# Row sums for the token groups by wide matmuls and 32 by 32 transposes, with the output groups taken in token order

## The chip, the cores and the metric

One core of one Trainium2 chip. The metric is the device time of one execution in microseconds (us); lower is better. The kernel before takes 180.8 us. Its executions agree within 0.3%, so a change of 0.5 us can be seen.

## The reference, cut to what matters

The program is a windowed attention followed by a "soft mixture of experts". Attention gives a matrix `x` of 4608 tokens (8 batches of 576) by 512. Then:

```python
logits = x @ phi                                  # 4608 x 32 slots
d = softmax of logits over the tokens             # axis 0
slot_out = for each expert e: relu((d.T @ x)[e] @ w1[e]) @ w2[e]     # 32 x 512
c = np.exp(logits - logits.max(1, keepdims=True))
c /= c.sum(1, keepdims=True) + 1e-09              # row sums: one per token
return (c @ slot_out).astype(np.float32)          # 4608 x 512
```

The change touches the last two lines: how the row sums of `c` are formed, and in which groups of 512 tokens the result is computed and stored.

## The kernel before

`o_et` holds `exp(logits)` transposed, 32 slots over the partitions and tokens along the free dimension. A small list scheduler in the kernel orders all operations; each gets a priority (`prio`, from the table `OFFS` and from `PERIOD`), and it keeps track of which operation reads or writes which buffer (`reads=`, `writes=`). The program gives each engine its instructions in the order that it finds.

The output is made in nine groups of 512 tokens. 576 is not a multiple of 512, so groups 0 to 7 are the first 512 tokens of each batch, and group 8 collects the last 64 tokens of all eight batches ("tail"). Its result goes back to eight places in the output:

```python
    op(POOL, lambda: pool.tensor_copy(                       # gather of the tail tokens
        a(o_tail, [[4, 8], [32, 16], [1, 4]]), a(o_et + 512, [[576, 8], [4, 16], [1, 4]])), ...)
    # row sums: a 33rd column in the matmul ET of each batch, and a matmul RS for the tail
    ...
    def tok(G, j):
        return (a(o_et + 576 * G + j, [[4, 128]]) if G < 8 else a(o_tail + j, [[4, 128]]))
    ...
    def store(G, c0, cw, prio, j0=0, n=4):
        ...
        if G < 8:
            dst = out[576 * G:576 * G + 512, c0:c0 + cw].rearrange("(p j) f -> p j f", j=4)[:, j0:j0 + n, :]
            src = af(ostg(G) + 2 * (512 * j0 + c0), [[512, n], [1, cw]])
        else:
            dst = out.rearrange("(b r) f -> b r f", b=8)[:, 512:576, :].rearrange("b (i j) f -> i b (j f)", j=4)
            src = af(ostg(G), [[1, 2048]])
        store_ops.append(op(SP, lambda: spq.dma_start(dst, src), ...))
    ...
    NA = 2.5         # the first 2.5 groups are stored by column halves, while the last weights land
    for G, x in [(2, 2)] + [(G, x) for G in (8, 3, 4, 5, 6, 7) for x in (0, 2)]:
        ...          # the other groups, 1 MB a store; group 8 goes first of the six
```

In every full store a partition holds four tokens, 8 KB that lie together in the output. For groups 0 to 7 the output side of the transfer is 128 pieces with one step. For group 8 it is 16 times 8 pieces: partition 8i+b goes to piece i of batch b.

The softmax here doesn't subtract the row's maximum and nothing guards it: scores larger than these inputs give would overflow.

## Time and profile before

| | before |
|---|---|
| time, median | 180.82 us |
| span of the profiled execution | 179.0 us |
| last weight packet ends | 152.3 us |
| loop over the attention ends, first L1 matmul | 129.2 us |
| 8 KB store packets: first start, last end | 160.45 us, 178.22 us |
| first 128 of them: mean duration | 518 ns |
| the others: median duration | 309 ns |

L1 and L2 are the first and the second matmul layer of the experts (`w1`, `w2`). The packet figures are read from the DMA records of the trace (start, size and duration of each packet of the queue that stores use), not from a printed view; the records do not say which of the 16 DMA engines moved a packet. The span of the profiled execution is 1.8 us shorter than its time.

The page shows the span in 40 slices. The DMA row is the busy share of the 16 DMA engines in tenths, the other what they moved in GB/s:

```profile
DMA  6999999999999999999999999999999999899996
GB/s 185 234 213 210 217 207 215 211 211 210 218 207 213 215 209 210 215 210 210 215 208 212 213 211 217 211 215 210 219 209 217 196 195 230 304 356 264 421 419 260
```

The DMA engines are busy from the first slice to the last (6 tenths in these two, 8 or 9 in all the others). While loading they write some 212 GB/s into the core; inputs are read as float32 and written as bfloat16, so an estimated 424 GB/s are read. The page's totals bear out the factor of about two: 61.93 MB read from HBM, 31.8 MB written into the core (41.26 MB moved less 9.44 MB of stores). In the stores at the end the rate reaches 421 GB/s, but one slice (161 to 165.6 us) has only 264.

The end of the chain of waits (start, duration, what):

```profile
120.53 32.06 DMA ar<-in_moe_w_dram
152.59 0.04 issue
152.63 0.30 PE ps L857
152.95 0.44 DVE ar L881
153.89 8.63 DVE ar L913 x15
```

The last load is waited for until 152.6 us; compute adds little after it, and then results are evicted and stored. The timeline of PE shows how much room the second layer (line 857) has:

```profile
136.14 4.28 PE L857 MATMUL ps<-ar 128*32 128x512 bf16 x44 [0.45 <-DVE ar L842]
141.93 1.04 PE L857 MATMUL ps<-ar 128*32 128x512 bf16 x4 [1.51 <-DMA ar<-in_moe_w_dram]
144.50 1.05 PE L857 MATMUL ps<-ar 128*32 128x256 bf16 x8 [1.53 <-DMA ar<-in_moe_w_dram]
```

In brackets is the idle time before each and what ended it: PE waits for weights, 1.51 and 1.53 us, so a microsecond more or less of compute before this costs nothing. Last, the windows view in the store phase; after the window and its length come the busy times of PE (the matmul engine), PEld (its weight loads), DVE (vector engine), ACT (scalar engine) and POOL (GpSimd), then the PE clock, the DMA share, and GB/s:

```profile
160.00:161.00 1.00, 0.96 (x4) 0.24 (x4) 1.00 (x2) 1.00 (x3) 0.00 (x0) 1.00 1.13 328
161.00:162.00 1.00, 0.93 (x5) 0.23 (x3) 1.00 (x3) 1.00 (x3) 0.00 (x0) 1.00 1.08 238
162.00:163.00 1.00, 0.33 (x1) 0.03 (x1) 1.00 (x2) 1.00 (x3) 0.00 (x0) 1.00 0.84 172
163.00:164.00 1.00, 0.00 (x0) 0.00 (x0) 1.00 (x3) 0.22 (x1) 0.00 (x0) 1.00 1.10 336
177.00:178.00 1.00, 0.00 (x0) 0.00 (x0) 0.00 (x0) 0.00 (x0) 0.00 (x0) 0.50 0.35 147
```

From 160 to 163 us the DMA engines are busy (a packet counts where it starts, so a share can pass 1: 1.13, 1.08, 0.84) but slow. That is when the first 1 MB store, group 8, runs.

### The profile page before, as it was taken

Reading aid. Unit: us, or ns where it says so; the run is one execution under the profiler, and the core shown is the slowest. Engines: PE = TensorE matmul, PEld = TensorE weight load, DVE = VectorE, ACT = ScalarE, POOL = GpSimd, SP = SyncE. Lnnn points to the kernel's source line nnn. Section 1 sums busy time; section 2 is a strip of 40 time slices with the busy share of each in tenths; the row PEclk is TensorE's granted clock in tenths of the full one; section 3 lists DMA queues with packets and bytes.
Section 4 is the critical chain, followed back from the end, with each engine's and each line's share of the span. In section 5 each row is a group of like instructions: output and inputs, shape, how many; then the busy total and the mean of one; then the engine's idle time right before and its main releaser. Section 6 shows DMA issues by size and latency. Waiting matters only on the chain.

```text
span 179.0 us, 4780 instructions
## 1 busy us (share of the span) xinstructions
PE 127.9 (71%) x2093; PEld 87.5 (49%) x2094; DVE 118.0 (66%) x220; ACT 104.7 (58%) x165; POOL 51.7 (29%) x103
## 2 busy tenths in 40 slices
PE   0009778989789989989699989976697657892000
PEld 0006556666567767767477767664444224420000
DVE  6898579788899899899589699383300015797000
ACT  2405299797789799798666889875111004694000
POOL 7559741332423432333930000790100000000000
PEclk9999999999999999999965999999879999999555
DMA  6999999999999999999999999999999999899996
GB/s 185 234 213 210 217 207 215 211 211 210 218 207 213 215 209 210 215 210 210 215 208 212 213 211 217 211 215 210 219 209 217 196 195 230 304 356 264 421 419 260
DMA packets 19220, 41.26 MB, mean 230 GB/s; under 512 B 1920, under 2 KB 8576, under 8 KB 18304
## 3 DMA queue, kind: packets, MB, share of 16 engines
q0 software_dynamic: 15056, 30.41, 90.0%
q1 hardware_dynamic: 4144, 10.55, 16.6%
q8 instruction: 16, 0.26, 0.5%
q14 instruction: 4, 0.03, 0.0%
HBM read 61.93 MB, written 9.44 MB: 399 GB/s over the span
## 4 chain that ended last, share of the span: by engine, by line
DMA 32%; PE 23%; DVE 23%; ACT 6%; POOL 4%; issue 2%; DVEq 0%
DMA ar<-in_moe_w_dram 18%; DMA ar<-in_k_dram 15%; PE ps L509 7%; DVE ar L488 6%; DVE ar L913 6%; ACT ar L548 4%; POOL ar L371 4%; PE ps L603 3%; DVE ar L614 3%; PE ps L570 3%; PE ps L516 2%; PE ps L526 2%; PE ps L693 2%; DVE ar L494 2%; DVE ar L445 2%
## 5 line engine op out<-in xcount | busy, mean ns | idle before, releaser
L548 ACT ACTIVATE ar<-ps 128x1152 bf16<-128x1152 f32 (+1 forms) x32 | 38.0, 1186 | 22.8 <-PE ps L533 12.5
L488 DVE STREAM_TRANSPOSE ar<-ar 128x576 uint32<-128x576 uint32 x40 | 48.4, 1240 | 3.1 <-DMA ar<-in_k_dram 2.9
L509 PE MATMUL ps<-ar 128*128 128x320 bf16 (+1 forms) x128 | 23.9, 313 | 15.4 <-DVE ar L488 13.1
L614 DVE TENSOR_TENSOR ar<-ps,fs 96x768 bf16<-96x768 f32 (+1 forms) x32 | 26.3, 823 | 1.2
L576 ACT ACTIVATE ar<-ps 128x768 bf16<-128x768 bf16 x32 | 24.8, 811 | 2.2 <-PE ps L570 2.2
L509 PEld LDWEIGHTS ps<-ar 128*128 128x128 bf16 x128 | 10.9, 102 | 20.1 <-POOL ar L418 13.1
L603 PE MATMUL ps<-ar 128*128 128x65 bf16 x320 | 15.7, 200 | 3.4 <-ACT ar L548 3.1
L570 PE MATMUL ps<-ar 128*128 128x128 bf16 x192 | 16.3, 232 | 2.2 <-DVE ar L614 1.9
L910 ACT ACTIVATE ar<-ps,fs 128x512 f32<-128x512 f32 (+1 forms) x23 | 11.4, 641 | 8.3 <-PE ps L901 8.3
L603 PEld LDWEIGHTS ps<-ar 128*128 128x128 bf16 x320 | 12.9, 101 | 6.3 <-ACT ar L548 3.8
L335 POOL DMA_DIRECT2D ar<-in_k_dram x16 | 8.9, 553 | 23.1 <-DVE ar L488 18.2
L610 DVE RECIPROCAL fs<-ps 96x12 f32<-96x12 f32 (+1 forms) x32 | 6.4, 200 | 12.6 <-PE ps L603 12.4
L570 PEld LDWEIGHTS ps<-ar 128*128 128x128 bf16 x192 | 12.8, 120 | 3.6 <-DVE ar L614 2.4
L857 PE MATMUL ps<-ar 128*32 128x512 bf16 (+1 forms) x80 | 10.5, 338 | 5.0 <-DMA ar<-in_moe_w_dram 3.5
L913 DVE TENSOR_SCALAR ar<-ps,fs 128x512 f32<-128x512 f32 (+1 forms) x23 | 12.7, 628 | 1.0 <-PE ps L901 1.0
L364 POOL DMA_DIRECT2D ar<-in_moe_w_dram x12 | 6.4, 580 | 22.2 <-DVE ar L488 22.2
L335 POOL DMA_DIRECT2D ar<-in_q_dram x16 | 8.7, 546 | 11.5 <-DVE fs L610 6.6
L335 POOL DMA_DIRECT2D ar<-in_v_dram x16 | 8.8, 549 | 9.2 <-DVE fs L610 5.5
L670 ACT ACTIVATE ar<-ps 128x576 bf16<-128x576 bf16 x16 | 9.6, 652 | 2.3 <-PE ps L654 2.3
L901 PE MATMUL ps<-ar 128*128 128x512 bf16 (+1 forms) x45 | 9.8, 339 | 1.5 <-DVE ar L881 1.0
L693 PE MATMUL ps<-ar 128*128 128x288 bf16 x64 | 9.2, 287 | 1.2 <-ACT ar L677 1.2
L857 PEld LDWEIGHTS ps<-ar 128*32 128x32 bf16 x80 | 4.7, 96 | 10.6 <-DMA ar<-in_moe_w_dram 6.8
(75 smaller groups left out, 192.6 us busy)
## 6 DMA issues: line engine op xcount, KB each, us to landing
ar<-in_moe_w_dram POOLq DMA_DIRECT2D x29, 512.0 KB, 27.2
out_dram<-ar SPq DMA_DIRECT2D x6, 1024.0 KB, 11.0
ar<-in_k_dram POOLq DMA_DIRECT2D x16, 288.0 KB, 21.8
ar<-in_q_dram POOLq DMA_DIRECT2D x16, 288.0 KB, 22.3
ar<-in_v_dram POOLq DMA_DIRECT2D x16, 288.0 KB, 22.3
out_dram<-ar SPq DMA_DIRECT2D x10, 256.0 KB, 3.8
ar<-in_moe_w_dram SPq DMA_DIRECT2D x1, 1024.0 KB, 4.9
ar<-in_moe_w_dram POOLq DMA_DIRECT2D x2, 256.0 KB, 31.7
```

The costliest lines, as they stand in the source:

```text
L335: return pool.dma_start(a(o_stg + (s * 3 + j) * 1152, [[1, 1152]]), src[b, 4 * dl:4 * dl + 4].rearrange("h (p t) d -> (h p) (t d)", p=32))
L488: return dve.transpose(au(o_dst, [[1, 18], [18, 32]]), au(src, [[32, 18], [1, 32]]))
L509: pe.matmul(pf(h, 0, [[1, W]]), a(o_id, [[1, 128]]), a(msk, [[1, W]]), start=True, stop=False)
L548: eo = op(ACT, lambda P=P, W=W: act.activation(a(P, [[W, 4], [1, W]]), AP(ps, 0, [[4096, 128], [512, 4], [1, W]]), ACTF.Exp, scale=SCALE), ...
L570: last = pe.transpose(pb(bank.idx, bb * 256 + par * 32, [[64, 4], [1, 32]]), src, a(o_id, [[1, 128]]))
L576: op(ACT, lambda t=t, bank=bank: act.activation(a(o_vb[vs] + 3 * t * VBK, [[66, 12], [2, 32], [1, 2]]), pb(bank.idx, 0, [[64, 12], [1, 32] ...
L603: last = pe.matmul(pf(bank.idx + x, 65 * t, [[1, 65]]), w, a(VB + t * VBK + 66 * h, [[1, 65]]), start=True, stop=True)
L614: op(DVE, lambda hp=hp, bank=bank: dve.tensor_tensor(a(ox + 128 * hp, [[64, 2], [256, NT], [1, 64]], 0, rows), pf(bank.idx, 0, [[512, 2], ...
L693: last = pe.matmul(pf(bank.idx, 0, [[1, 288]]), a(o_phis + 128 * c, [[1, 128]]), a(o_xt[xt] + 576 * c + 288 * g, [[1, 288]]), start=(c == ...
L857: last = pe.matmul(pf(sobank[x].idx, 0, [[1, n]], 32 * j, 32), a(o_htz + 1024 * g + 128 * c + 32 * j, [[1, 32]]), a(w2off(e) + DM * c + co ...
L910: op(ACT, lambda: act.activation(dst, src(), ACTF.Copy, scale=sca), actt(cw, .1), prio + .1, reads=[bank, b_rinv], writes=wr, name=f"OE{G} ...
L913: op(DVE, lambda: dve.tensor_scalar(dst, src(), sca, None, op0=AluOp.mult), dvet(cw, True) + .08, prio + .1, reads=[bank, b_rinv], writes= ...
```

## The change

The intent: take groups of 512 consecutive tokens over the borders of the batches, so that the gather, the tail buffer and the scattered store go. The row sums then no longer fit the batches. They are made three groups at a time: four matmuls of 384 columns, each to its own 32 partitions, with weights of 32 equal columns, so that every output row is the row sum; a 32 by 32 transpose on DVE is to bring the tokens into the partitions. `OFFS` and `PERIOD`, the priorities of the scheduler, were retuned.

```diff
-PERIOD = 20.3
+PERIOD = 21.8
-OFFS = dict(T=54.1, SC=81.0, EX=-15.2, MK=68.9, ...)
+OFFS = dict(T=92.2, SC=104.1, EX=-30.5, MK=78.7, ...)
 ...
-                last = pe.matmul(pf(bank.idx, 33 * t, [[1, 33]]), w, a(o_sel, [[1, 33]]),
+                last = pe.matmul(pf(bank.idx, 32 * t, [[1, 32]]), w, a(o_sel, [[1, 32]]),
 ...
-        op(DVE, lambda bank=bank: dve.reciprocal(
-            f(o_rinv + 4 * b, [[1, 4]]), pf(bank.idx, 33 * 6 + 32, [[33, 4]])), ...)
 ...
+    def row_sums(g0, g1, prio):
+        ...
+                for qd in range(4):
+                    last = pe.matmul(pf(bank.idx + m, 0, [[1, 384]], 32 * qd, 32), a(o_rm, [[1, 32]]),
+                                     a(o_et + 512 * (g0 + 3 * m) + 128 * qd, [[512, 3], [1, 4], [4, 32]]),
+                                     start=True, stop=True)
+        op(PE, fn, pet(4 * n, 384), prio, reads=[b_et, b_rm], writes=[bank], name=f"RS{g0}")
+        op(DVE, lambda: dve.transpose(af(o_rt, [[384, n], [1, 384]]), pf(bank.idx, 0, [[512, n], [1, 384]])), ...)
+        op(DVE, lambda: dve.reciprocal(f(o_rinv + 4 * g0, [[1, 12 * n]]), af(o_rt, [[32, 12 * n]])), ...)
 ...
+        if i in (9, 13):
+            row_sums(0 if i == 9 else 3, 3 if i == 9 else 6, 15 * PERIOD)
 ...  (tail gather, RS and RR8 removed)
+    row_sums(6, 9, T1 + 4)
 ...
-        if G < 8:
-            dst = out[576 * G:576 * G + 512, c0:c0 + cw].rearrange(...)
-        else:
-            dst = out.rearrange("(b r) f -> b r f", b=8)[:, 512:576, :].rearrange("b (i j) f -> i b (j f)", j=4)
+        dst = out[512 * G:512 * G + 512, c0:c0 + cw].rearrange("(p j) f -> p j f", j=4)[:, j0:j0 + n, :]
 ...
-    for G, x in [(2, 2)] + [(G, x) for G in (8, 3, 4, 5, 6, 7) for x in (0, 2)]:
+    for G, x in [(2, 2)] + [(G, x) for G in range(3, 9) for x in (0, 2)]:
```

More of the change, by code (lines that the diff above doesn't have):

```diff
@@ L26 @@
 LRU = 130.0
-OFFS = dict(T=54.1, SC=81.0, EX=-15.2, MK=68.9, TB=-27.8, VE=-19.3, PV=-25.0, RC=-26.6,
-            NM=-144.9, XT=-17.3, XE=7.3, LG=-85.5, EXL=22.3, ET=33.1, EE=23.9, SI=46.0, SA=37.9)
+OFFS = dict(T=92.2, SC=104.1, EX=-30.5, MK=78.7, TB=-29.0, VE=-46.3, PV=-36.7, RC=-26.4,
+            NM=-241.3, XT=-17.7, XE=8.2, LG=-77.2, EXL=95.9, ET=37.3, EE=30.2, SI=61.8, SA=58.7)
 class Buf:
@@ L240, in bass_dilated_sliding_attn__then__soft_moe_slots_kernel @@
     o_id = take(128)
-    o_sel = take(34)
-    o_rm = o_sel + 32
+    o_sel = take(32)
+    o_rm = take(32)
+    o_rt = take(768)
     o_so = take(512)
-    o_tail = take(512)
     o_htz = take(2 * 8 * 4 * 32)
@@ L310, in bass_dilated_sliding_attn__then__soft_moe_slots_kernel @@
     b_w2h = [[Buf(f"w2h{x}{s}") for s in range(2)] for x in range(4)]
-    b_htz, b_tail, b_so = Buf("htz"), Buf("tail"), [Buf("soA"), Buf("soB")]
+    b_htz, b_rt, b_so = Buf("htz"), Buf("rt"), [Buf("soA"), Buf("soB")]
     b_hsb = [Buf(f"hsb{x}") for x in range(2)]
@@ L457, in const_ops @@
            reads=[b_sel], writes=[b_rm])
+        op(DVE, lambda: dve.tensor_copy(a(o_rm + 1, [[1, 31]]), a(o_rm, [[0, 31]])), .1, D0 + 1, rmw=[b_rm])
     const_ops()
@@ L720, in half @@
         ek = b % 2
-        op(PE, et_fn, pet(11, 33), pr("ET"), reads=[b_et, b_sel, b_rm], writes=[bank], name=f"ET{b}")
-        ee = op(ACT, lambda bank=bank: act.activation(
-            a(o_ek[ek], [[32, 11], [1, 32]]), pf(bank.idx, 0, [[33, 11], [1, 32]]), ACTF.Copy), actt(352),
-           pr("EE"), reads=[bank], writes=[b_ek[ek]], name=f"EE{b}")
-        op(DVE, lambda bank=bank: dve.reciprocal(
-            f(o_rinv + 4 * b, [[1, 4]]), pf(bank.idx, 33 * 6 + 32, [[33, 4]])), .2, pr("EE") + .1,
-           reads=[bank], writes=[b_rinv], after=[ee], name=f"RR{b}")
+        op(PE, et_fn, pet(11, 32), pr("ET"), reads=[b_et, b_sel], writes=[bank], name=f"ET{b}")
+        op(ACT, lambda bank=bank: act.activation(
+            a(o_ek[ek], [[1, 352]]), pf(bank.idx, 0, [[1, 352]]), ACTF.Copy), actt(352), pr("EE"),
+           reads=[bank], writes=[b_ek[ek]], name=f"EE{b}")
         bank = Bank(f"si{b}")
@@ L750, in half, with fn @@
            rmw=[b_sid] if b < 7 else [], writes=[b_sdb] if b == 7 else [], name=f"SD{b}")
-    def tok(G, j):
-        return (a(o_et + 576 * G + j, [[4, 128]]) if G < 8 else
-                a(o_tail + j, [[4, 128]]))
+    def row_sums(g0, g1, prio):
+        n = (g1 - g0) // 3
+        bank = Bank(f"rs{g0}", n)
+        def fn():
+            last = None
+            for m in range(n):
+                for qd in range(4):
+                    last = pe.matmul(pf(bank.idx + m, 0, [[1, 384]], 32 * qd, 32), a(o_rm, [[1, 32]]),
+                                     a(o_et + 512 * (g0 + 3 * m) + 128 * qd, [[512, 3], [1, 4], [4, 32]]),
+                                     start=True, stop=True)
+            return last
+        op(PE, fn, pet(4 * n, 384), prio, reads=[b_et, b_rm], writes=[bank], name=f"RS{g0}")
+        op(DVE, lambda: dve.transpose(af(o_rt, [[384, n], [1, 384]]), pf(bank.idx, 0, [[512, n], [1, 384]])),
+           .1 + .4 * n, prio + .1, reads=[bank], writes=[b_rt], name=f"RT{g0}")
+        op(DVE, lambda: dve.reciprocal(f(o_rinv + 4 * g0, [[1, 12 * n]]), af(o_rt, [[32, 12 * n]])),
+           .2, prio + .2, reads=[b_rt], writes=[b_rinv], name=f"RR{g0}")
     last_ex = [None]
@@ L794, in bass_dilated_sliding_attn__then__soft_moe_slots_kernel @@
        reads=[bank], writes=[b_sit], name="sid")
-    op(POOL, lambda: pool.tensor_copy(
-        a(o_tail, [[4, 8], [32, 16], [1, 4]]), a(o_et + 512, [[576, 8], [4, 16], [1, 4]])), .8, T1 + 4, reads=[b_et],
-       writes=[b_tail], name="tail")
-    bank = Bank("rs")
-    def rs_fn(bank=bank):
-        last = None
-        for j in range(4):
-            last = pe.matmul(pf(bank.idx, j, [[1, 1]]), tok(8, j), a(o_rm, [[1, 1]]),
-                             start=True, stop=True)
-        return last
-    op(PE, rs_fn, pet(4, 72), T1 + 4, reads=[b_tail, b_rm], writes=[bank], name="RS")
-    op(DVE, lambda bank=bank: dve.reciprocal(f(o_rinv + 32, [[1, 4]]), pf(bank.idx, 0, [[1, 4]])),
-       .2, T1 + 4.2, reads=[bank], writes=[b_rinv], name="RR8")
+    row_sums(6, 9, T1 + 4)
     for x in range(2):
@@ L900, in out_tile @@
         rd = [b_so[s] for s in range(2) if c0 < 256 * (s + 1) and c0 + cw > 256 * s]
-        op(PE, lambda: pe.matmul(pf(bank.idx, 0, [[1, cw]]), tok(G, j),
+        op(PE, lambda: pe.matmul(pf(bank.idx, 0, [[1, cw]]), a(o_et + 512 * G + j, [[4, 128]]),
                                  a(o_so + c0, [[1, cw]]), start=True, stop=True),
-           pet(1, cw), prio, reads=[b_et if G < 8 else b_tail] + rd, writes=[bank], name=f"O{G}{j}{c0}")
+           pet(1, cw), prio, reads=[b_et] + rd, writes=[bank], name=f"O{G}{j}{c0}")
         dst = af(ostg(G) + 2 * (512 * j + c0), [[1, cw]])
@@ L919, in store @@
               if c0 < 256 * (s + 1) and c0 + cw > 256 * s]
-        if G < 8:
-            dst = out[576 * G:576 * G + 512, c0:c0 + cw].rearrange("(p j) f -> p j f", j=4)[:, j0:j0 + n, :]
-            src = af(ostg(G) + 2 * (512 * j0 + c0), [[512, n], [1, cw]])
-        else:
-            dst = out.rearrange("(b r) f -> b r f", b=8)[:, 512:576, :].rearrange("b (i j) f -> i b (j f)", j=4)
-            src = af(ostg(G), [[1, 2048]])
+        dst = out[512 * G:512 * G + 512, c0:c0 + cw].rearrange("(p j) f -> p j f", j=4)[:, j0:j0 + n, :]
+        src = af(ostg(G) + 2 * (512 * j0 + c0), [[512, n], [1, cw]])
         store_ops.append(op(SP, lambda: spq.dma_start(dst, src), .1, prio, kind="dma",
@@ L939, in bass_dilated_sliding_attn__then__soft_moe_slots_kernel @@
         store(G, 256, 256, T2 + 10 + G + .25 * x + .2, x, 2)
-    for G, x in [(2, 2)] + [(G, x) for G in (8, 3, 4, 5, 6, 7) for x in (0, 2)]:
-        at = G if G < 8 else 2.6
+    for G, x in [(2, 2)] + [(G, x) for G in range(3, 9) for x in (0, 2)]:
         for j in (x, x + 1):
-            out_tile(G, j, 0, 512, T2 + 10 + at + .1 * x)
+            out_tile(G, j, 0, 512, T2 + 10 + G + .1 * x)
         if G < NA:
-            store(G, 0, 512, T2 + 10 + at + .1 * x + .1, x, 2)
+            store(G, 0, 512, T2 + 10 + G + .1 * x + .1, x, 2)
         elif x:
-            store(G, 0, 512, T2 + 10 + at + .3)
+            store(G, 0, 512, T2 + 10 + G + .3)
     order = sc.run([4, 5, 6, 7], [0, 1, 2, 3], last_ex[0])
```

## The prediction

> **What bounds the kernel now.** The DMA queues, nearly from first to last. In the page's 40 slices the DMA row is at 9 between the first slice and the last, except one 8. The windows view gives 212 GB/s into the core from 10 to 140 us (written as bf16, so about 424 GB/s read as float32), 191 to 196 GB/s in the column slabs of the last two experts, then 410 to 440 GB/s of stores. [...] The chain of waits says the same: its last loading step is a weight DMA, 120.5 to 152.6 us, then L2, eviction, stores. The timeline ends the compute loop about 128 us; L2 of the first experts is done at 140.4, then waits 1.5 us for weights at 141.9 and again at 144.5. So compute has slack: over 1 us in the tail, far more in the loop, where a load takes 22 us from issue to landing.
>
> **What the change does.**
> - PE: ET gets 32 instead of 33 columns (nothing). Twelve matmuls of 384 columns with 32 output rows come, four at a time over the array's columns. L1, the same form, does 64 of 512 columns in 4.97 us, so my estimate is 0.7 us in all[...]. The old RS (0.30 us) goes.
> - DVE: eight reciprocals of 0.16 to 0.18 us go; three transposes of 128x384 come, 0.8 us each by an estimate from 1.16 us for 128x576, and three small reciprocals. Net about +1.5 us, 0.9 us of it after the loop, where DVE waits anyway.
> - POOL: the 0.63 us gather of the tail tokens goes. It was off the chain.
> - The loop's order is retuned. I expect its end to move by up to 2 us, the load end not at all.
> - Stores: still six of 1 MB and eleven smaller, but the ninth group is no longer 128 pieces of 8 KB scattered over eight batches. This is on the critical path. In the trace's DMA records the 8 KB store packets take 309 ns in the median; the first 64, from 160.45 us, about 600 to 640 ns, and 32 of the next 64 about 530. By issue order these 128 are the scattered group. Their excess, over 16 engines, is 1.7 us; throughput at 162 to 163 us falls to 172 GB/s. [...]
>
> **Sum.** Load end unchanged, 152.6 us. Stores from 160.4 us: six times 2.46 us plus what is left of contention, ending about 176.5 instead of 178.2. Everything else is hidden. Predicted 179.2 us, range 178.2 to 180.9. Faster by over 2%: 0.03; within 2%: 0.94; slower by over 2%: 0.03.
>
> **What would show it.** 8 KB store packets at 309 ns from the first on; no slice under 300 GB/s between 160 and 164 us; last weight landing within 0.5 us of 152.6; L2 still waiting for weight DMA; RS under 1.5 us of PE; three transposes about 0.8 us each.
>
> **What would make it wrong.** (1) The slow packets come from the evictions beside them until 164.5 us, not from the scattered rows: then the next group is slow and nothing is gained (about 180.8). (2) The last row sums land before the last slot sums and push L1 and L2 past the weights: over 1.5 us shows as later first stores. (3) The row sums read the buffer that the next batch's exponentials write, so they stall the loop; over several us this starves the load queue.

Stores from 160.4 us, six times 2.46 us (128 packets of 309 ns over 16 engines are 2.47), and by difference 1.3 us for what is left of contention, end at 176.5 us. In the kernel before, the last store packet ends at 178.22 us in the trace and the time is 180.82; with these 2.6 us the sum comes to 179.1.

## The result, and the profile after

The kernel after takes 178.31 us (median of 4 runs, 178.13 to 178.71) against 180.85 us. The ratio is 0.986, 95% interval 0.984 to 0.988. Ratios here are the mean time of one kernel's fast runs over that of the other's fast runs of the same rounds, so not quite the ratio of the medians quoted. All these runs are fast (an execution over 1.5% above the fastest of its kernel is called slow and left out).

| | before | after |
|---|---|---|
| span | 179.0 us | 176.3 us |
| first L1 matmul | 129.2 us | 128.1 us |
| last weight packet ends | 152.3 us | 152.2 us |
| 8 KB store packets: first start, last end | 160.45, 178.22 us | 160.32, 175.54 us |
| first 128 of them: mean duration | 518 ns | 318 ns |
| sum of all their durations, over 16 engines | 16.83 us | 15.13 us |

The same lines after. First the slices:

```profile
DMA  5999999999999999999999999999999999999997
GB/s 182 237 211 213 216 207 213 214 209 213 215 208 214 214 208 214 214 207 215 210 209 213 211 211 216 213 216 210 217 213 211 210 192 194 298 319 415 416 427 316
```

The slice of 264 GB/s is gone; from 158.7 us on all but the last are at 415 or more. The chain of waits has the same end, at the same times, within 0.1 us:

```profile
119.16 33.35 DMA ar<-in_moe_w_dram
152.51 0.04 issue
152.56 0.30 PE ps L858
152.88 0.44 DVE ar L882
153.81 8.63 DVE ar L914 x15
```

So at most 0.13 us was gained before the stores: the first 8 KB packet starts at 160.32 instead of 160.45 us. The windows of the store phase:

```profile
154.00:155.00 1.00, 1.00 (x8) 0.66 (x7) 1.00 (x4) 1.00 (x4) 0.00 (x0) 1.00 0.59 206
160.00:161.00 1.00, 0.96 (x4) 0.16 (x3) 1.00 (x2) 1.00 (x3) 0.00 (x0) 1.00 1.11 455
161.00:162.00 1.00, 0.93 (x4) 0.26 (x3) 1.00 (x3) 1.00 (x3) 0.00 (x0) 1.00 0.99 401
162.00:163.00 1.00, 0.25 (x1) 0.00 (x0) 1.00 (x2) 1.00 (x3) 0.00 (x0) 1.00 1.05 434
163.00:164.00 1.00, 0.00 (x0) 0.00 (x0) 1.00 (x3) 0.16 (x1) 0.00 (x0) 1.00 0.99 410
```

DVE still evicts at full load until 164 us and ACT until 163 us, and still the stores run at over 400 GB/s. The added work, from the groups by shape (busy time and mean of one in ns, then idle time before it):

```profile
L760 PE MATMUL ps<-ar 128*32 128x384 bf16 x12 | 1.7, 501 | 0.0
L766 DVE STREAM_TRANSPOSE ar<-ps 128x384 f32<-128x384 f32 x3 | 1.7, 571 | 1.9 <-PE ps L760 1.9
L768 DVE RECIPROCAL fs<-ar 128x12 f32<-128x12 f32 x3 | 0.7, 222 | 0.1
```

The four matmuls of a set overlap; a set takes 0.51 us, three sets 1.5 us. Other forecasts held too: the last weight lands at 152.2 us, and L2 still waits for weight DMA (1.23 us before 141.77 us, by the timeline).

Two things call for an explanation. The sum of the packets' durations fell by 1.70 us (16.83 - 15.13), as predicted, but the stretch from the first to the last of them fell by 2.55 us (17.77 - 15.22). And nothing so far says why the scattered store was slow.

### The profile page after: what moved, and what is told of

Same layout as the page of the kernel before. It is cut to its first block, busy times and chain, and to the rows that moved or that the text cites. A ratio compares the mean times of both kernels' runs of the same rounds, so it can differ in the third digit from the quotient of the medians.

```text
span 176.3 us, 4802 instructions
## 1 busy us (share of the span) xinstructions
PE 126.7 (72%) x2102; PEld 85.4 (48%) x2102; DVE 119.6 (68%) x218; ACT 104.3 (59%) x165; POOL 51.1 (29%) x102
## 4 chain that ended last, share of the span: by engine, by line
DMA 47%; DVE 21%; PE 13%; POOL 4%; ACT 4%; issue 2%; POOLq 0%; DVEq 0%
DMA ar<-in_k_dram 28%; DMA ar<-in_moe_w_dram 19%; DVE ar L489 6%; DVE ar L914 6%; PE ps L510 4%; POOL ar L371 3%; ACT ar L549 3%; PE ps L604 2%; DVE ar L615 2%; PE ps L571 2%; DVE ar L445 2%; PE ps L517 2%; DVE ar L450 1%; PE ps L527 1%; DVE ar L495 1%
## 5 line engine op out<-in xcount | busy, mean ns | idle before, releaser
L510 PE MATMUL ps<-ar 128*128 128x320 bf16 (+1 forms) x128 | 23.4, 308 | 15.7 <-DVE ar L489 13.8
L510 PEld LDWEIGHTS ps<-ar 128*128 128x128 bf16 x128 | 10.4, 100 | 20.8 <-POOL ar L418 13.7
L571 PE MATMUL ps<-ar 128*128 128x128 bf16 x192 | 15.8, 228 | 2.8 <-DVE ar L615 1.9
L604 PEld LDWEIGHTS ps<-ar 128*128 128x128 bf16 x320 | 12.8, 100 | 6.5 <-ACT ar L549 3.8
L858 PE MATMUL ps<-ar 128*32 128x512 bf16 (+1 forms) x80 | 11.4, 352 | 5.9 <-DMA ar<-in_moe_w_dram 5.2
L571 PEld LDWEIGHTS ps<-ar 128*128 128x128 bf16 x192 | 12.4, 118 | 4.3 <-DVE ar L615 2.5
L902 PE MATMUL ps<-ar 128*128 128x512 bf16 (+1 forms) x46 | 10.4, 356 | 1.3 <-DVE ar L882 1.0
```

The lines of the kernel that those rows point to most:

```text
L510: pe.matmul(pf(h, 0, [[1, W]]), a(o_id, [[1, 128]]), a(msk, [[1, W]]), start=True, stop=False)
L571: last = pe.transpose(pb(bank.idx, bb * 256 + par * 32, [[64, 4], [1, 32]]), src, a(o_id, [[1, 128]]))
L604: last = pe.matmul(pf(bank.idx + x, 65 * t, [[1, 65]]), w, a(VB + t * VBK + 66 * h, [[1, 65]]), start=True, stop=True)
L858: last = pe.matmul(pf(sobank[x].idx, 0, [[1, n]], 32 * j, 32), a(o_htz + 1024 * g + 128 * c + 32 * j, [[1, 32]]), a(w2off(e) + DM * c + co ...
L902: op(PE, lambda: pe.matmul(pf(bank.idx, 0, [[1, cw]]), a(o_et + 512 * G + j, [[4, 128]]), a(o_so + c0, [[1, cw]]), start=True, stop=True), ...
```

## The experiments

Theory S: the whole gain comes from the store of the ninth group; the rest of the change is neutral. Rivals: E, the evictions beside the first 1 MB store made it slow; R, the new row sums and order have a part. On why the store is slow: A, its addresses are far apart; P, its form, that is, which partition goes to which piece (16 times 8 instead of one step of 128), wherever the pieces lie.

Five of the kernels below (`b_contig`, `a_scatter`, `b_perm`, `b_pitch`, `b_pitchperm`) put rows in the wrong order. The comparison with the reference passed them all the same: the rows of this result differ little (any entry is within 3.1e-5 of its column's mean, where the largest entry is 4.4e-4), so it cannot see the order of rows. For the kernels that are called correct here, the kernel after among them, the order rests on reading the code.

### 1. Before, with contiguous stores

```diff
-        if G < 8:
-            dst = out[576 * G:576 * G + 512, ...]
-        else:
-            dst = out.rearrange(...)           # the eight places
+        dst = out[512 * G:512 * G + 512, c0:c0 + cw].rearrange("(p j) f -> p j f", j=4)[:, j0:j0 + n, :]
```

> The kernel before, with every group's store at a contiguous 1 MB of the output (rows 512G to 512G+511), all else as before; the result is wrong on purpose. Theory S (the scattered rows of the ninth group's store are the whole gain): 178.1 to 178.6 us, 8 KB store packets at 309 ns from the first on, and the last ones end within 0.5 us of one another. Rival E (the evictions that run beside the first 1 MB store slow it, wherever it goes): 180.8 us, first 128 packets still slow. Rival R (part of the gain comes from the rest of the change): about 179.2 us, the gain from the packets' mean excess alone (1.7 us).

Measured: 178.37 us, ratio to before 0.9859 (0.9842 to 0.9875), the same as the kernel after. One of its four executions took 369.8 us and counts as slow; the profile fell on it, so of this kernel only the three fast times (178.14 to 178.49) are used. What the forecast says of single packets could therefore not be checked in it. With nothing but the stores changed, the whole gain is there. For the ninth group that is two things at once, its addresses and the form of the transfer (one step of 128 instead of 16 times 8); experiments 4 to 6 take them apart.

### 2. After, with the stores addressed as before

```diff
+        if G != 3:
+            at = 576 * (G if G < 3 else G - 1)
+            dst = out[at:at + 512, ...]
+        else:
+            dst = out.rearrange(...)           # the eight places
```

> The kernel after, with its stores addressed as before: the first 1 MB group goes to the eight 64-row holes, the others to rows 576k; the result is wrong on purpose. Theory S: 180.6 to 181.0 us, the first 128 packets of 8 KB at about 600 ns. Rival E: unchanged, 178.3 us. Rival R: about 180.0 us, since the new row sums and the new order keep their part.

Measured: 180.74 us against 180.77, ratio 0.9996 (0.9981 to 1.0011). The first 64 packets of 8 KB have a median of 624 ns, and the windows view shows the slow stretch again:

```profile
162.00:163.00 1.00, 0.25 (x1) 0.00 (x0) 1.00 (x2) 1.00 (x3) 0.00 (x0) 1.00 0.99 229
```

The new row sums, the new order and the missing gather together are worth nothing that these runs can tell; S stands, R and E fall.

### 3. Before, with the scattered group last

```diff
-    for G, x in [(2, 2)] + [(G, x) for G in (8, 3, 4, 5, 6, 7) for x in (0, 2)]:
-        at = G if G < 8 else 2.6
+    for G, x in [(2, 2)] + [(G, x) for G in (3, 4, 5, 6, 7, 8) for x in (0, 2)]:
+        at = G
```

> The kernel before, the scattered group stored last of the six instead of first; correct result. Theory S: the slow packets move to the end of the stores (after 175 us), the first 1 MB store is at 309 ns; the time stays at 180.8 or grows by up to 1 us[...]. Rival E: the first 1 MB store (now a contiguous one) stays slow, the scattered one is at 309 ns, time 180.8 us.

Measured: 180.09 us, ratio 0.9958 (0.9943 to 0.9973), result correct. The slow packets went with the group: the first 128 take 318 ns in the mean, the last 128 take 487. The windows view, beside the evictions and long after them:

```profile
162.00:163.00 1.00, 0.23 (x1) 0.00 (x0) 1.00 (x2) 1.00 (x2) 0.00 (x0) 1.00 1.03 426
174.00:175.00 1.00, 0.00 (x0) 0.00 (x0) 0.00 (x0) 0.00 (x0) 0.00 (x0) 0.50 1.03 188
```

E is refuted a second time: the first store is fast beside the evictions, and the last is slow where none runs. It got 0.7 us faster, not slower as I had thought possible: the packets add up to less (16.61 us over 16 engines instead of 16.83), and an engine is idle for less of the last 2.5 us (0.34 us in the mean instead of 0.81). Why less unevenness is left when the slow store comes last stays open.

### 4. Contiguous stores, the ninth group's pieces in the order of the scattered store

```diff
+        else:
+            dst = out[4096:4608, :].rearrange("(b i j) f -> i b (j f)", b=8, j=4)
```

> As b_contig, but the ninth group writes its contiguous 1 MB with the access pattern of the scattered store: partition 8i+b to piece b*16+i, so consecutive partitions are 128 KB apart instead of 1.18 MB; wrong result on purpose. If the order in which pieces go to the DMA engines is what costs: 180.8 us and slow packets as before. If the large distance costs: 178.3 us and 309 ns.

Measured: 180.92 us, ratio 1.0009 (0.9993 to 1.0026), and a median of 628 ns in the first 64 packets. The windows view:

```profile
162.00:163.00 1.00, 0.20 (x1) 0.00 (x0) 1.00 (x3) 1.00 (x2) 0.00 (x0) 1.00 0.94 229
```

So all the pieces can lie within one contiguous 1 MB and the store is as slow as when spread over 9.4 MB. Rows far apart are not what it takes. But 128 KB and 1.18 MB are both multiples of 128 KB, so a rule about distances was not yet out; hence the next two.

### 5. Every group scattered, in one step of 128; and the same addresses as 16 times 8

```diff
-        if G < 8: ... else: ...
+        dst = out.rearrange("(p g j) f -> g p j f", g=9, j=4)[G][:, j0:j0 + n, c0:c0 + cw]
```

> The kernel before, with every group scattered over the whole output: piece p of group G goes to rows 36p+4G to 36p+4G+3, so consecutive partitions are 72 KB apart, but the access pattern still has one outer dimension of 128; wrong row order on purpose. Theory P ([...] distance in the output costs nothing): 178.1 to 178.6 us, 8 KB packets at 309 ns. Rival A (scattered output addresses cost): 8 KB packets well over 309 ns in all six groups, and over 181 us.

The second kernel differs from it in the ninth group alone, which covers the same pieces in another order:

```diff
+        else:
+            dst = out.rearrange("(b i g j) f -> g i b (j f)", b=8, g=9, j=4)[G]
+            src = af(ostg(G), [[1, 2048]])
```

> As b_pitch, with the same set of addresses, but the ninth group in the 16 times 8 order: partition 8i+b goes to piece 16b+i. Theory P: 180.6 to 181.0 us, 128 slow packets of about 600 ns, the other groups at 309 ns. Rival A: the same time as b_pitch, whatever that is.

Measured: 178.31 us, ratio 0.9869 (0.9854 to 0.9883), with every group scattered, and 181.07 us, ratio 1.0016 (0.9999 to 1.0032), with the ninth in the 16 times 8 order. The windows view of the first:

```profile
161.00:162.00 1.00, 0.93 (x5) 0.21 (x3) 1.00 (x3) 1.00 (x3) 0.00 (x0) 1.00 0.99 401
162.00:163.00 1.00, 0.35 (x1) 0.05 (x1) 1.00 (x2) 1.00 (x3) 0.00 (x0) 1.00 0.99 410
```

and of the second:

```profile
161.00:162.00 1.00, 0.96 (x4) 0.15 (x2) 1.00 (x3) 1.00 (x3) 0.00 (x0) 1.00 1.06 246
162.00:163.00 1.00, 0.47 (x2) 0.11 (x1) 1.00 (x3) 1.00 (x3) 0.00 (x0) 1.00 0.90 164
```

The set of addresses is the same, and the rate in the last column falls from 401 to 246 and from 410 to 164 GB/s. Theory A in its plain form is refuted: it is not where the pieces lie, but which partition goes to which piece, that is, how the transfer is described. One rule about distances is still not out by this pair: from one partition to the next the 16 times 8 order jumps 1.18 MB again, the fast one 72 KB. Experiment 6 holds the addresses fixed.

### 6. The ninth group in eight stores, reading partitions 8 apart or next to each other

If P is right, then it should matter from which partitions a store reads its pieces, while the addresses that it writes stay the same. What the runs show so far is a factor of about two: the first 64 packets have a median of 613 ns in the kernel before, 624 in `a_scatter` and 628 in `b_perm`, against 309 ns. In the two windows from 161 to 163 us, with the slow store, `a_scatter` moved 205 and 229 GB/s, `b_perm` 213 and 229, and the kernel before 238 and 172, where the kernel after moved 401 and 434.

These two kernels, both correct, write identical addresses in eight stores of sixteen pieces; only the partitions differ: sixteen partitions 8 apart, or sixteen neighbours. (The figures for P in the two expectations are my estimates.)

```diff
+        if G == 8:
+            for b in range(8):      # one store for each batch
+                spq.dma_start(out[576 * b + 512:576 * b + 576, :].rearrange("(i j) f -> i (j f)", j=4), SRC)
 # b_st8: SRC = partitions b, b+8, b+16, ... (the gather as before: 8i+b)
 # b_st1: SRC = partitions 16b to 16b+15      (the gather changed to 16b+i)
```

> The kernel before, correct result, the ninth group's store cut into eight of 128 KB, one for each batch, each reading sixteen partitions 8 apart (8i+b). [...] Theory P: packets of 500 to 620 ns in this group, 180.3 to 181.3 us. Rival A: the same addresses as before, so as before too; the pair with b_st1 tells.

> As b_st8, same addresses and same eight stores, correct result, but each reads sixteen neighbouring partitions (16b+i)[...]. Theory P: packets of about 900 to 1200 ns in this group, and 1 to 5 us slower than b_st8. Rival A: the same time as b_st8.

Measured: 180.49 us (ratio 0.9985, 0.997 to 1.0) and 181.25 us (1.0032, 1.0017 to 1.0047). The packets, from the DMA records:

| kernel | first 1 MB of 8 KB packets | first 16 packets, median | first 128, mean | time |
|---|---|---|---|---|
| after | one store, one step of 128 | 309 ns | 318 ns | 178.31 us |
| b_pitch | one store, one step of 128 | 309 ns | 318 ns | 178.31 us |
| before | one store, 16 times 8 | 534 ns | 518 ns | 180.8 us |
| b_pitchperm | one store, 16 times 8 | 567 ns | 520 ns | 181.07 us |
| b_st8 | eight stores, partitions 8 apart | 495 ns | 494 ns | 180.49 us |
| b_st1 | eight stores, neighbouring partitions | 1096 ns | 577 ns | 181.25 us |

The first sixteen packets, as many as there are engines, start at about the same time (within 0.44 us in the kernel before). In the 16 times 8 stores and in `b_st8` their median is 1.6 to 1.8 times 309 ns, in `b_st1` 3.5 times; the slowest of `b_st1` took 1309 ns, 4.2 times. Among its later packets many take 309 ns again, and the mean of the first 128 evens out at 577 ns; `b_st1` is only 0.8 us slower than `b_st8`, where I had expected 1 to 5. The trace does not name the engine of a packet, so how the pieces were shared out among the engines is not shown. But no theory that looks at addresses or sizes alone tells these two kernels apart, and the forecast for P gave their order and, for the first packets, about their durations (495 ns for 500 to 620, 1096 ns for 900 to 1200). The sixteen pieces of each of these stores adjoin in the output (128 KB in all), and the first sixteen packets of `b_st8` are slow all the same, so a rule about jumps does not explain them. So it is shown that, at fixed addresses, the partitions that a store reads matter; why they do, and that the same thing is behind the factor of about 2 of the 16 times 8 store, is not shown. The most direct test, a contiguous store described as 16 times 8 in its plain order, is not among the runs, nor is a store with jumps of 128 KB or 1.18 MB in one step.

The windows view of `b_st8` (two lines) and of `b_st1` (the last):

```profile
161.00:162.00 1.00, 0.93 (x4) 0.26 (x3) 1.00 (x3) 1.00 (x3) 0.00 (x0) 1.00 0.83 180
163.00:164.00 1.00, 0.00 (x0) 0.00 (x0) 1.00 (x3) 0.17 (x1) 0.00 (x0) 1.00 0.77 246
161.00:162.00 1.00, 0.97 (x4) 0.15 (x2) 1.00 (x2) 1.00 (x3) 0.00 (x0) 1.00 0.41 123
```

The times of these two say less than their packets. From 0.8 us after the first to 2.5 us before the last of the 8 KB packets an engine is idle for 0.48 us in the mean in `b_st8` and for 0.32 us in `b_st1`, in the kernel before for none; and of the 0.8 us between the two, 0.34 us lie before the first 8 KB packet (160.33 and 160.67 us in the profiled runs).

The unequal waiting also answers the first question above. The records show when packets end: in the kernel before six packets are under way at 177.5 us, two at 178.0, and the last ends at 178.22. In the kernel after 16 are under way at 175.0 and all are done by 175.54. In the last 2.5 us of the stores an engine is idle for 0.81 us in the mean before, and for 0.10 us after. That is 0.71 of the 0.85 us (2.55 - 1.70) to be explained; another 0.10 us is idle time at the start. The slow store left the engines at different places, and the one that is last ends the kernel.

### 7. After, with the old order

```diff
-PERIOD = 21.8
+PERIOD = 20.3
-OFFS = dict(T=92.2, ...)
+OFFS = dict(T=54.1, ...)     # as in the kernel before
```

> The kernel after with the priorities and the period of the kernel before (the retuned order undone, all else kept); correct. If the retuned order has no part in the gain, as predicted: 178.1 to 178.7 us, as the kernel after. If it has: up to 180 us.

Measured: 185.55 us (median of the three fast runs, 184.71 to 186.43; a fourth, 188.11, counts as slow), ratio 1.0259 (1.0216 to 1.0303): slower than either kernel, and against my expectation. The stores are fast in it (393 to 451 GB/s from 167 to 179 us), but late (the first is issued at 157.84 us). Its timeline:

```profile
129.21 0.51 PE L760 MATMUL ps<-ar 128*32 128x384 bf16 x4 [0.16 <-ACT ar L577]
129.79 0.41 ACT L702 ACTIVATE ar<-ps 128x288 bf16<-128x288 f32 x1
145.39 3.64 PE L819 MATMUL ps<-ar 128*32 128x512 bf16 x64 [0.32 <-DVE ar L808]
```

and that of the kernel after:

```profile
97.30 0.52 PE L760 MATMUL ps<-ar 128*32 128x384 bf16 x3
97.51 0.50 PE L760 MATMUL ps<-ar 128*32 128x384 bf16 x1
100.46 0.41 ACT L702 ACTIVATE ar<-ps 128x288 bf16<-128x288 f32 x1
128.13 3.64 PE L819 MATMUL ps<-ar 128*32 128x512 bf16 x64 [0.32 <-DVE ar L808]
```

Line 760 is the first set of row sums, line 702 the exponential of batch 5. The row sums read `b_et`, and that one name stands for the whole buffer of all batches, so the next exponential, which writes another part of it, may not start before they are done. The row sums have a low priority; in the old order they came at 129.2 us, and the exponential of batch 5 started 0.07 us after their end, instead of at 100.5. With it the loop ended late: L1 (line 819) began at 145.4 us instead of 128.1. The last weight had landed at 152.3 us as always, but in the old order nothing was ready to be stored. The windows view of this kernel:

```profile
154.00:155.00 1.00, 1.00 (x17) 0.65 (x13) 0.00 (x0) 0.00 (x0) 0.00 (x0) 1.00 0.00 0
```

PE is the bottleneck there and the DMA engines stand still. Not all of the delay is put down to the row sums: the exponential of batch 4, before any of them, already came at 92.7 us (85.8 in the kernel before), PE already stood idle for 2.9 us before 110.5 us in this kernel, waiting for DVE, and how much of the 17 us each has was not separated.

### 8. After, with the row sums done twice

```diff
         if i in (9, 13):
-            row_sums(0 if i == 9 else 3, 3 if i == 9 else 6, 15 * PERIOD)
+            for _ in range(2):
+                row_sums(0 if i == 9 else 3, 3 if i == 9 else 6, 15 * PERIOD)
 ...
     row_sums(6, 9, T1 + 4)
+    row_sums(6, 9, T1 + 4)
```

> The kernel after with the row sums done twice (24 wide matmuls, 6 transposes, 6 reciprocals); correct. If they lie off the critical path, as predicted: within 0.3 us of the kernel after, 178.0 to 178.8 us, though PE and DVE are busy about 1.5 and 2.4 us longer. If they are on it: at least 1 us slower.

Measured: 180.16 us, ratio to before 0.9969 (0.9934 to 1.0003), 1.85 us slower than the kernel after (180.16 - 178.31, not run side by side). It does not measure what it was meant to. The first set came at 98.35 us, but its copy at 122.65, and the exponential of batch 5 started at 123.23, when the copy was done. It is the same false dependence as in 7 (both sets come before that exponential in the program); what the doubled work itself costs stays open.

### 9. Two tries at a faster kernel

Expert 6 loaded whole, only expert 7 in column slabs:

```diff
-    for e in range(6):
+    for e in range(7):
         wq += [w2_piece(e, 0), w2_piece(e, 4)]
-        wq += [w2_slab(6, s), w2_slab(7, s, 0, 4), ...]
+        wq += [w2_slab(7, s, 0, 4), ...]
```

> A try at a faster kernel: the kernel after, with W2 of expert 6 loaded in two whole pieces like experts 0 to 5 instead of two column slabs, so that only expert 7 comes in the small 512-byte packets; correct. From the windows of the profile, slabs run at 195 GB/s and whole pieces at 212: half the slab bytes (1.05 MB) at the better rate save an estimated 0.4 us; the first stores start up to 2 us later, but they then fill the gap at 154 us. Theory: 177.5 to 178.1 us. Rival (a later start of the stores leaves the queues idle): 178.3 us or slower.

Measured: 180.62 us, 2.3 us slower than the kernel after (not run side by side). The loads end earlier as hoped, at 151.9 instead of 152.2 us. But the timeline has the first store at 153.01 us instead of 149.34, 3.7 us later where I had allowed 2, since all of expert 6 lands before the first slab of expert 7. The windows view of this kernel shows the hole:

```profile
152.00:153.00 1.00, 1.00 (x8) 0.72 (x7) 0.50 (x2) 0.69 (x2) 0.00 (x0) 0.85 0.00 0
153.00:154.00 1.00, 1.00 (x10) 0.74 (x9) 1.00 (x3) 1.00 (x4) 0.00 (x0) 1.00 0.05 17
```

Three groups instead of two and a half stored by column halves:

```diff
-    NA = 2.5
+    NA = 3
-    for G, x in [(2, 2)] + [(G, x) ...]:
+    for G, x in [(G, x) ...]:
```

> A second try: the kernel after, with three groups instead of two and a half stored by column halves, so that more stores are ready while the last weights land and the DMA share of 0.59 at 154 to 155 us is filled; correct. Against it: 0.5 MB more goes in 1 KB packets, at 46 ns for 1 KB against 309 for 8 KB, an estimated 0.2 us. Expected 178.0 to 178.5 us.

Measured: 177.72 us (177.62 to 177.88), below what I had expected, correct, ratio to before 0.9826 (0.9812 to 0.9841). It was not run side by side with the kernel after, but its slowest run is faster than the fastest of that one (178.13), and the kernel before took 180.85 us beside each; so it beats the kernel before and, as far as runs apart can tell, the kernel after by 0.6 us. The windows view of this kernel, where the kernel after has a share of 0.59:

```profile
154.00:155.00 1.00, 1.00 (x9) 0.66 (x7) 1.00 (x3) 1.00 (x4) 0.00 (x0) 1.00 0.80 282
```

More stores were ready when the loads ended. The last 8 KB packet ends at 175.12 us instead of 175.54.

## Why the prediction was right or wrong

The time fell in the range, but only 0.1 us above its lower end: 178.31 us against 179.2 (178.2 to 180.9). The gain was 2.5 us where 1.65 had been forecast. The path was right (the ninth group's store, on the DMA engines); its size was not, and the reason for the slow store had been left open. The points:

- The DMA engines bound the kernel, and the loads end where they did: right. The chain waits for the last weight until 152.5 us, before 152.6.
- The gain is in the ninth group's store: right, and shown from both sides. The store side alone, addresses and form together, brings the gain to the kernel before (178.37), and takes it from the kernel after (180.74).
- "Their excess, over 16 engines, is 1.7 us": right as a sum (1.70 us), wrong as the time gained. This is the term that was mis-sized. I subtracted the mean over the engines, ending at 176.5 us; the kernel ends with its last engine, and the stretch of the stores shrank by 2.55 us, ending at 175.54. Of the 0.85 us between, 0.71 is idle time of engines in the last 2.5 us, the unevenness that the slow store left behind; and the stores began 0.13 us earlier.
- The cause: left open between the scattered rows and the evictions. The runs speak against both: a pitch of 72 KB in all groups cost nothing (178.31 us), and beside the evictions the packets of a plain store take 318 ns in the mean, against 314 ns for the last 128 of the kernel after, where none runs. What every slow single store has in common is the 16 times 8 form (medians of 613 to 628 ns in the first 64 packets of before, `a_scatter`, `b_perm` and `b_pitchperm`); why that form is slow is not shown. The prediction's packet figures were rough: in the records 31 of the first 64 lie between 590 and 660 ns, and the slow half of the next 64 has a mean of about 550 and a median of 571.
- Added work: the matmuls take 1.5 us, twice my estimate (0.7) and just over the limit that I had set ("under 1.5"). The 0.7 us had been scaled from L1's 4.97 us, which ran at a granted clock of 0.72; in the kernel after, at 1.00, L1 takes 3.64 us, so the same scaling gives 0.5 us, and the row sums took three times that. One of them, 384 columns with a moving operand of stride 4, lasts 498 ns (median), one of L1, 512 columns without a stride, 379 ns; that the stride is the cause was not tested by itself, and the ends of matmuls are modelled in the trace. The transposes take 0.57 us, not 0.8. Neither shows in the time.
- "I expect its end to move by up to 2 us": right for the loop's end (129.2 to 128.1 us), but treating the retuning as a side matter was wrong. Without it the same change takes 185.6 us. That the order handed in with the change was a good one was luck as far as the prediction goes. The danger was my point (3), the row sums that hold up the next exponentials; the retuned order avoids it by running the first set at 97.3 us, before the exponential of batch 5 is due.
- Point (2), the last row sums delaying L1: did not happen; L1 began 1.1 us earlier.

## What to carry to other kernels

A store from 128 partitions is not fast by its size alone (180.92 us in `b_perm` and 178.37 us in `b_contig`, where the ninth group's 1 MB has the same address): where the far side needs two dimensions for the partitions, compare the durations of its packets with those of a plain store of the same packet size, and choose the groups so that one step does. When a phase is bound by 16 engines, estimate its end from the slowest of them, not from the mean (here the mean gave 1.70 us, and the stretch of the stores shrank by 2.55). And when work is added off the critical path, look at which buffer names it reads: a coarse name makes it a barrier, and then the order decides whether it is free.
